# One layout of 6 tokens on 96 partitions for q, k and v, with exps and packed products written contiguously

## The chip, the cores and the metric

The kernel runs on 1 core of one Trainium2 chip. The metric is the device time of one execution in microseconds; a trace's "span" is the time from the first to the last instruction, some 2 us shorter. The engines are TensorE (PE; its weight loads are shown as PEld), VectorE (DVE), ScalarE (ACT), GpSimd (POOL) and SyncE (SP). PSUM is the memory in which this kernel's matmuls leave their results, SBUF holds its other tiles, and an eviction is an instruction of VectorE or ScalarE that reads PSUM and writes SBUF. A packet is one record of the trace's DMA part. A run over 1.5% above the fastest of the same kernel is called slow. Fast runs are compared with fast runs.

## The reference

```python
batch, n_heads, seq, head_dim = (8, 8, 576, 64)      # q, k, v; p has 32 rows in place of 576
def sm_attn(qq, kk, vv):
    s = scale * np.matmul(qq, kk.transpose(0, 1, 3, 2))
    ...                                              # softmax over the last axis
    return np.matmul(a, vv)
p_packed = sm_attn(p, k, v)
out = sm_attn(q, p_packed, p_packed)
x = out.transpose(0, 2, 1, 3).reshape(B * S, H * D)  # 4608 tokens x 512
h = x @ w_in                                         # w_in 512 x 2048
g = h * np.cos(h)
return g @ w_out                                     # w_out 2048 x 512, result float32
```

## The kernel before

The kernel works batch by batch. Because `p_packed` has only 32 rows per head, it multiplies these rows with `w_in` first: the "packed products" `PPW`, 128 rows x 2 groups x 2048 columns per batch. The second softmax gives `a2n`, and `h` is one matmul of `PPW` with `a2n`. The output projection of the batch before (`ot`) is used as filler: `fill(n)` puts n of its matmuls between other work of TensorE.

The parts that the change touches:

```python
def load(n, b):                      # cast to bf16 during the transfer
    if n == "q":                     # 128 partitions, 9216 bytes of float32 each, in one piece
        t = x[n, b] = ld_pool.tile([128, S * H * D // 128], BF16, name="q_bf", tag=n)
        G.dma_start(out=t, in_=q[b].rearrange("h (r t) d -> (h r) (t d)", r=QG))
    else:                            # 96 partitions, 6 tokens of each head
        t = x[n, b] = ld_pool.tile([KP, H, KC * D], BF16, name=n + "_bf", tag=n)
        G.dma_start(out=t, in_=src[n][b].rearrange("h (p c) d -> p h (c d)", c=KC))

def load_w_out(n):                   # 4 rows of w_out, 8 KB, in one piece
    G.dma_start(out=w_out_bf[:, 4 * n:4 * n + 4, :],
                in_=moe_w_out.rearrange("(n m j) d -> m n j d", n=4, j=4)[:, n])
...
def ppw_piece(b, n, engs):           # a quarter of the packed products
    ...                              # 8 matmuls into ps[0], ps[1]
    for g in range(2):
        dst = PPW[b][:, g, n * 512:(n + 1) * 512].rearrange("p (j m) -> p m j", j=4)
        src_ = ps[g].rearrange("p (m j) -> p m j", j=4)
        ...                          # dst = src_ * rinv, on VectorE or ScalarE
...
def s2_exp(b, g):
    dst = a2u[b][:, g].rearrange("p (r t o) -> p o t r", r=QG, o=2)
    for o in range(2):
        A.activation(out=dst[:, o], in_=ps[o], func=AF.Exp, ...)
```

`PPW` is written with 256 bytes between neighbouring elements of the inner loop (128 bf16 elements), the exps with 72 bytes (36 elements). The loads stand in one queue in this order: k, v, q of batch 0; `w_in`; the rest of p; `w_out`; k, q, v of batch 1; k, q, v of batch 2. k and q of batch 0 are transposed by TensorE (`pe_T`), all later ones by a transposing DMA (`dma_T`), issued by SyncE. TensorE works in program order, so after batch 0 it stands still until the transpose of k of batch 1 ("kT(1)") has landed:

```python
dma_T("k", 1)
dma_T("q", 1)
...                                  # batch 0: h, sin, g
dma_T("k", 2)
set_filler(0)
exp_table()
fill(16)
for i in range(3):
    s1_mm(1, i)                      # the first matmuls that read kT(1)
    s1_exp(1, i)
```

The softmax here doesn't subtract the row's maximum and nothing guards it: scores larger than these inputs give would overflow.

Of the kernel before, what the change touches and what calls it, by code (L numbers as in the profile page):

```python
# [8 lines left out]
FP32 = mybir.dt.float32  # L9
BF16 = mybir.dt.bfloat16  # L10
AF = mybir.ActivationFunctionType
ALU = mybir.AluOpType
# [4 lines left out]
def kernel(  # L17
# [14 lines left out]




    nc = tc.nc
    B, H, S, D = q.shape
    DM, DF = moe_w_in.shape
    scale = 1.0 / (D ** 0.5)
    NFC = DF // 128  # L40
    KP, KC = 96, S // 96
    QG, QB = 128 // H, S * H // 256
    PSUM = bass.MemoryType.PSUM

    const = ctx.enter_context(tc.tile_pool(name="const", bufs=1))
    ld_pool = ctx.enter_context(tc.tile_pool(name="ld", bufs=2))
    T_pool = ctx.enter_context(tc.tile_pool(name="T", bufs=2))
# [8 lines left out]
    work = ctx.enter_context(tc.tile_pool(name="work", bufs=5, space=PSUM))  # L56
# [4 lines left out]
    V, A, G = nc.vector, nc.scalar, nc.gpsimd  # L61
# [4 lines left out]
    ident = const.tile([128, 128], BF16, name="ident")  # L66
# [7 lines left out]
    src = {"k": k, "q": q, "v": v}  # L74
# [3 lines left out]
    x, xT = {}, {}  # L78

    def load(n, b):  # L80
        if n == "q":
            t = x[n, b] = ld_pool.tile([128, S * H * D // 128], BF16, name="q_bf", tag=n)
            G.dma_start(out=t, in_=q[b].rearrange("h (r t) d -> (h r) (t d)", r=QG))
        else:
            t = x[n, b] = ld_pool.tile([KP, H, KC * D], BF16, name=n + "_bf", tag=n)
            G.dma_start(out=t, in_=src[n][b].rearrange("h (p c) d -> p h (c d)", c=KC))

    def load_w_in(c0, c1):
        G.dma_start(out=w_in_bf[:, :, c0:c1], in_=moe_w_in.rearrange("(a p) n -> p a n", p=128)[:, :, c0:c1])

    def load_w_out(n):
        G.dma_start(out=w_out_bf[:, 4 * n:4 * n + 4, :],
                    in_=moe_w_out.rearrange("(n m j) d -> m n j d", n=4, j=4)[:, n])

    def copy(eng, out, in_):
        if eng is A:
            A.copy(out=out, in_=in_)  # L97
        else:
            eng.tensor_copy(out=out, in_=in_)  # L99


    def T_tile(n, b):
        w = 128 if n == "q" else KP
        t = xT[n, b] = T_pool.tile([128, H * S // (2 * w), w], BF16, name=n + "T", tag=n + "T")
        return t, (x[n, b] if n == "q" else x[n, b].rearrange("p h x -> p (h x)")), w

    def dma_T(n, b):
        t, f, w = T_tile(n, b)
        nc.sync.dma_start_transpose(out=t, in_=f)

    def pe_T(n, b, engs):
        t, f, w = T_tile(n, b)
        nb = f.shape[-1] // 128
        for i, j0 in enumerate(range(0, nb, 8)):
            m = min(8, nb - j0)
            ps = work.tile([128, m, w], BF16, name="tps", tag="w")
            for j in range(m):
                nc.tensor.transpose(ps[:, j, :], f[:, (j0 + j) * 128:(j0 + j + 1) * 128], ident[0:w, 0:w])
            copy(engs[i % len(engs)], t[:, j0:j0 + m, :], ps)

    def pack_p(b0, b1):

# [12 lines left out]
    a2u, a2n, PPW, rinv, ppT, lns = {}, {}, {}, {}, {}, {}  # L135
    s1_ps, s2_ps = {}, {}
# [35 lines left out]
    def ppw_piece(b, n, engs):  # L172
        if b not in PPW:
            PPW[b] = ppw_pool.tile([128, 2, DF], BF16, name="PPW", tag="PPW")
        ps = [work.tile([128, 512], FP32, name="ppw", tag="w") for _ in range(2)]
        for hp in range(4):
            for o in range(2):
                r = slice(64 * o, 64 * o + 64)
                nc.tensor.matmul(ps[o][32 * hp:32 * hp + 32], ppT[b][r, 2 * hp + o, :],  # L179
                                 w_in_bf[r, hp, n * 512:(n + 1) * 512], start=True, stop=True,  # L180
                                 tile_position=(64 * o, 32 * hp))
        for g in range(2):
            dst = PPW[b][:, g, n * 512:(n + 1) * 512].rearrange("p (j m) -> p m j", j=4)
            src_ = ps[g].rearrange("p (m j) -> p m j", j=4)
            s = rinv[b][:, 2 * g:2 * g + 1]
            if engs[g] is A:
                A.activation(out=dst, in_=src_, func=AF.Copy, scale=s)  # L187
            else:
                engs[g].tensor_scalar(out=dst, in0=src_, scalar1=s, scalar2=None, op0=ALU.mult)  # L189

    def s2_mm(b, g):

        ps = s2_ps[b, g] = [work.tile([128, QB, QG], FP32, name="s2", tag="w") for _ in range(2)]
        for hp in range(4):
            for o in range(2):
                r = slice(64 * o, 64 * o + 64)
                h = 2 * hp + g
                nc.tensor.matmul(ps[o][32 * hp:32 * hp + 32], ppT[b][r, h, :],
                                 xT["q", b][r, :, QG * h:QG * h + QG],
                                 start=True, stop=True, tile_position=(64 * o, 32 * hp))  # L200

    def s2_exp(b, g):
        ps = s2_ps.pop((b, g))
        if b not in a2u:
            a2u[b] = a2_pool.tile([128, 2, S], BF16, name="a2u", tag="a2u")
        dst = a2u[b][:, g].rearrange("p (r t o) -> p o t r", r=QG, o=2)
        for o in range(2):
            A.activation(out=dst[:, o], in_=ps[o], func=AF.Exp, scale=rinv[b][:, 2 * g + 1:2 * g + 2])  # L208

    def sums(b, i):  # L210

# [17 lines left out]

    gT, joint, ht, h_open = {}, {}, {}, {}  # L230

    def h_mm(b, fc):


        if fc == 0:
            gT[b] = g_pool.tile([128, NFC, 512], BF16, name="gT", tag="gT")
            if b % 2 == 0:
                joint[b // 2] = g_pool.tile([128, NFC, 128], BF16, name="joint", tag="joint")
        ps = h_open[b, fc] = work.tile([128, 512], FP32, name="hT", tag="w")
        for g in range(2):  # L240
            nc.tensor.matmul(ps, PPW[b][:, g, fc * 128:(fc + 1) * 128],  # L241
                             a2n[b][:, g, 0:512], start=(g == 0), stop=(g == 1))
        j = fc % 8
        for jj in {2: (0, 1), 3: (2, 3)}.get(j, (j,) if j > 3 else ()):
            if jj == 0:
                ht[b] = t_ps.tile([128, 8, 64], FP32, name="ht", tag="ht")
            f0 = (fc - j + jj) * 128
            for g in range(2):
                nc.tensor.matmul(ht[b][:, jj, :], PPW[b][:, g, f0:f0 + 128],  # L249
                                 a2n[b][:, g, 512:576], start=(g == 0), stop=(g == 1))  # L250

    def h_sin(b, fc):
# [14 lines left out]

    n_out = [0]

    def out_gen(b):  # L270
        chunks = [(gT[b], i) for i in range(4)]
        if b % 2 == 1:
            chunks.insert(0, (joint[b // 2], None))
        for t, i in chunks:
            x0 = 0 if i is None else i * 128
            ps = o_ps.tile([128, DM], FP32, name="ot", tag="ot")
            for fc in range(NFC):
                nc.tensor.matmul(ps, t[:, fc, x0:x0 + 128], w_out_bf[:, fc, :],  # L278
                                 start=(fc == 0), stop=(fc == NFC - 1))
                if fc < NFC - 1:  # L280
                    yield
            osb = o_pool.tile([128, DM], FP32, name="osb")
            copy(V if n_out[0] % 2 == 0 else A, osb, ps)
            n_out[0] += 1
            if i is None:
                nc.sync.dma_start(out=out[(b - 1) * S + 512:b * S, :], in_=osb[0:64, :])
                nc.sync.dma_start(out=out[b * S + 512:(b + 1) * S, :], in_=osb[64:128, :])
            else:
                nc.sync.dma_start(out=out[b * S + i * 128:b * S + (i + 1) * 128, :], in_=osb)
            yield  # L290

    filler = [None, 0]
# [14 lines left out]


    load("k", 0)
    nc.sync.dma_start(out=p_raw[:, 0:2, :], in_=p_rows[:, 0:2, :])  # L310
    make_identity(nc, ident)
    load("v", 0)
    load("q", 0)
    load_w_in(0, 512)
    load_w_in(512, DF)
# [28 lines left out]
    for g in range(2):  # L344
        s2_mm(0, g)
        s2_exp(0, g)
    ppw_piece(0, 0, [V, V])
    for i in range(3):
        sums(0, i)
    normalise(0)  # L350
    dma_T("k", 1)
    dma_T("q", 1)


# [6 lines left out]
    pack_p(1, 4)  # L361
    pack_p(4, 8)
    dma_T("k", 2)


# [8 lines left out]
    for g in range(2):  # L374
        s2_mm(1, g)
        s2_exp(1, g)
# [31 lines left out]
    def exp_phase(s, b2, b1):  # L408
        exp_table()
        s2_exp(b2, 0)  # L410
        s2_mm(b2, 1)
        s2_exp(b2, 1)
        fill(3)
        for i in range(3):
            if b1 is not None:
                s1_mm(b1, i)
                s1_exp(b1, i)
            fill(4)
        for i in range(3):
            sums(b2, i)  # L420
            fill(2)
        normalise(b2)
        h_mm(s, 8)
        fill(3)
        h_mm(s, 9)
        fill(3)
# [59 lines left out]
```

## Time and profile before

| | before |
|---|---|
| median of 3 runs | 337.89 us (336.65 to 340.62) |
| span of the profiled run | 336.1 us |
| first matmul on kT(1) | 60.2 us |
| first h matmul of batch 1 | 86.1 us |
| start of the exps of batches 2 to 7 | 99.5, 135.9, 170.2, 204.1, 237.9, 272.3 us |

From the page of the kernel before: busy us, share of the span and instructions of each engine, and the shares of the chain of work that ended last.

```profile
PE 264.1 (79%) x2226; PEld 127.6 (38%) x2226; DVE 210.5 (63%) x276; ACT 262.3 (78%) x298; POOL 22.5 (7%) x37
...
PE 30%; ACT 30%; DMA 17%; DVE 15%; issue 7%; POOL 1%; ACTq 0%; POOLq 0%; DVEq 0%
```

Two engines are about equally busy and the chain is spread over four kinds of work, so the page alone names no single limit. The groups of instructions (line, engine, operation, output<-inputs, shapes, count | busy us, mean ns of one | idle time before) show what is expensive:

```profile
L278 PE MATMUL ot<-w_out_bf,gT 128*128 128x512 bf16 x512 | 135.3, 386 | 0.0
L256 ACT ACTIVATE cosT<-hT,pihalf 128x512 bf16<-128x512 f32 x128 | 89.2, 740 | 15.9 <-PE hT L241 14.0 <-DVE gT L257 1.6
...
L189 DVE TENSOR_SCALAR PPW<-ppw,rinv 128x512 bf16<-128x512 f32 x34 | 84.3, 2524 | 6.0 <-PE ppw L179 6.0
...
L187 ACT ACTIVATE PPW<-ppw,rinv 128x512 bf16<-128x512 f32 x30 | 76.2, 2574 | 4.6 <-PE ppw L179 4.4
...
L99 DVE COPY osb<-ot 128x512 f32<-128x512 f32 x18 | 12.4, 688 | 19.3 <-PE ot L278 19.3
```

A packed product of 128x512 takes 2.5 us, while a plain copy of the same size out of PSUM (`osb`) takes 0.69 us. The exps of 128x288 are as slow for their size. One of the 32 from the instructions of their line (count: duration in ns min/median/max):

```profile
L208 ACT ACTIVATE a2u<-s_321,rinv x1: 1746/1746/1746, 21.2 to 21.2; 128x288 bf16<-128x288 f32 x1
```

The median of the 32 is 1.73 us. These durations overlap: within a group of four, one exp starts mostly 1.24 us after the other.

The chain of waits in order of time (start us, us, what), a few of its pieces:

```profile
14.15 23.93 DMA k_bf<-in_k_dram
38.09 22.03 DMA kT<-k_bf
...
62.30 4.29 PE ot L278 x12
...
80.51 6.96 DVE PPW L189 x3
...
99.46 5.25 ACT a2u L208 x4
...
313.94 18.14 PE ot L278 x84
```

The first 60 us are one load and one transpose. After that the a2u exps and the PPW products stand in the chain again and again. Three stages, from the start of the exps of one batch to that of the next (from:to in us and length, then busy us and instructions of PE, PEld, DVE, ACT, POOL, then granted clock, DMA share, GB/s):

```profile
170.20:204.10 33.90, 30.03 (x270) 14.48 (x269) 24.21 (x31) 32.62 (x39) 1.36 (x2) 1.00 0.63 121
204.10:237.90 33.80, 30.80 (x272) 14.88 (x271) 24.38 (x32) 32.66 (x38) 0.00 (x0) 1.00 0.33 67
237.90:272.30 34.40, 30.16 (x266) 14.50 (x265) 24.28 (x32) 32.51 (x38) 0.00 (x0) 1.00 0.22 56
```

ScalarE is busy about 32.6 of 34 us; TensorE about 30.2. At the start-to-start pitch of its matmuls TensorE's work in a stage needs about 27.6 us (an estimate from the pitches in this trace).

Two answers of the DMA view (packets, megabytes, share of 16 engines) for q0, the queue of the loads, and q1, the queue of transposes and stores: first q0 from 20 to 36 us, when only loads run; then both from 46 to 54 us, when the transpose of k(1) runs beside loads.

```profile
q0 software_dynamic: 1450, 3.51, 109.1%
```

The answer for 46 to 54 us, q0 and q1:

```profile
q0 software_dynamic: 747, 1.02, 92.5%
q1 hardware_dynamic: 751, 0.19, 33.9%
```

Load packets and transpose packets come in equal numbers there.

### The profile page before, as it was taken

What the parts mean: (1) busy time and instruction counts of PE and PEld (TensorE: products, weight loads), DVE (VectorE), ACT (ScalarE), POOL (GpSimd) and SP (SyncE); (2) the same over time, 40 slices, a digit from 0 to 9 for tenths busy, and PEclk for the clock granted to TensorE, in tenths of its full rate; (3) what the DMA queues carried; (4) which work ended last, traced back from release to release, by engine and by line L of the source; (5) the groups of instructions that cost most, each with busy time, mean ns of one, the idle gap of its engine ahead of it and who ended that gap; (6) DMA issues with size and microseconds to landing.
All of it is one profiled execution on the core that took longest, in us unless ns stands there. A gap on an engine that the chain in (4) does not pass through costs nothing.

```text
span 336.1 us, 5402 instructions
## 1 busy us (share of the span) xinstructions
PE 264.1 (79%) x2226; PEld 127.6 (38%) x2226; DVE 210.5 (63%) x276; ACT 262.3 (78%) x298; POOL 22.5 (7%) x37
## 2 busy tenths in 40 slices
PE   1835734865769478899889888998898879999995
PEld 1801222431335133454345334543443434444442
DVE  1367993066980989169925992599349934866400
ACT  1378980279999889999999989999999997966300
POOL 8112000110100200001001000000000000000000
PEclk9999799599699769999999999999999998999999
DMA  8999999999931990146867651514040011010131
GB/s 116 211 230 213 205 160 135 187 214 219 167 54 57 181 178 8 26 115 122 172 130 136 113 111 56 82 53 101 34 103 31 33 31 63 33 62 35 61 94 62
DMA packets 53703, 36.90 MB, mean 110 GB/s; under 512 B 34112, under 2 KB 46912, under 8 KB 53680
## 3 DMA queue, kind: packets, MB, share of 16 engines
q0 software_dynamic: 15456, 18.81, 34.5%
q1 hardware_dynamic: 38224, 17.76, 24.2%
q8 instruction: 17, 0.28, 0.3%
q14 instruction: 6, 0.05, 0.0%
HBM read 37.22 MB, written 9.44 MB: 139 GB/s over the span
## 4 chain that ended last, share of the span: by engine, by line
PE 30%; ACT 30%; DMA 17%; DVE 15%; issue 7%; POOL 1%; ACTq 0%; POOLq 0%; DVEq 0%
PE ot L278 18%; ACT a2u L208 10%; DVE PPW L189 8%; DMA k_bf<-in_k_dram 7%; PE hT L241 7%; DMA kT<-k_bf 7%; ACT PPW L187 6%; ACT cosT L256 4%; DVE gT L257 4%; DMA q_bf<-in_q_dram 3%; ACT a1T L147 2%; DVE ppT L168 2%; ACT lns L218 2%; ACT L256 2%; PE ppw L179 1%
## 5 line engine op out<-in xcount | busy, mean ns | idle before, releaser
L278 PE MATMUL ot<-w_out_bf,gT 128*128 128x512 bf16 x512 | 135.3, 386 | 0.0
L256 ACT ACTIVATE cosT<-hT,pihalf 128x512 bf16<-128x512 f32 x128 | 89.2, 740 | 15.9 <-PE hT L241 14.0
L257 DVE TENSOR_TENSOR gT<-hT,cosT 128x512 bf16<-128x512 f32 x128 | 88.8, 729 | 15.3 <-ACT cosT L256 14.8
L241 PE MATMUL hT<-a2n,PPW 128*128 128x512 bf16 x256 | 81.0, 405 | 15.3 <-ACT PPW L187 8.1
L189 DVE TENSOR_SCALAR PPW<-ppw,rinv 128x512 bf16<-128x512 f32 x34 | 84.3, 2524 | 6.0 <-PE ppw L179 6.0
L187 ACT ACTIVATE PPW<-ppw,rinv 128x512 bf16<-128x512 f32 x30 | 76.2, 2574 | 4.6 <-PE ppw L179 4.4
L278 PEld LDWEIGHTS <-gT 128*128 128x128 bf16 x512 | 44.0, 100 | 50.9 <-issue 15.9
L224 DVE TENSOR_TENSOR a2n<-a2u,lns 128x576 bf16<-128x576 bf16 x16 | 11.4, 755 | 52.4 <-ACT lns L222 52.4
L241 PEld LDWEIGHTS <-PPW 128*128 128x128 bf16 x256 | 24.3, 101 | 46.0 <-issue 16.4
L179 PE MATMUL ppw<-w_in_bf,ppT 64*32 64x512 bf16 x256 | 20.5, 419 | 18.3 <-ACT PPW L187 9.5
L249 PEld LDWEIGHTS <-PPW 128*128 128x128 bf16 x256 | 21.2, 100 | 24.6 <-issue 3.3
L97 ACT COPY osb<-ot 128x512 f32<-128x512 f32 x18 | 11.9, 659 | 16.4 <-PE ot L278 16.4
L99 DVE COPY osb<-ot 128x512 f32<-128x512 f32 x18 | 12.4, 688 | 19.3 <-PE ot L278 19.3
L249 PE MATMUL ht<-a2n,PPW 128*128 128x64 bf16 x256 | 23.6, 195 | 0.0
L168 DVE CAST ppT<-pp 64x128 bf16<-64x128 f32 x32 | 9.4, 294 | 17.0 <-PE pp L161 16.6
L142 PEld LDWEIGHTS <-kT 128*96 128x96 bf16 x192 | 13.4, 141 | 16.5 <-issue 6.8
L179 PEld LDWEIGHTS <-ppT 64*32 64x32 bf16 x256 | 6.1, 90 | 30.2 <-issue 22.5
L278 PE MATMUL ot<-w_out_bf,joint 128*128 128x512 bf16 x64 | 17.2, 392 | 0.0
L217 PE MATMUL sm<-a2u,ones_blk 128*128 128x384 bf16 x24 | 8.4, 360 | 8.2 <-ACT a2u L208 8.2
L218 ACT ACTIVATE lns<-sm 128x384 f32<-128x384 f32 x24 | 10.8, 514 | 0.8 <-PE sm L217 0.8
L261 ACT ACTIVATE cosTt<-ht,pihalf 128x512 bf16<-128x512 f32 x16 | 11.1, 691 | 0.0
L263 DVE TENSOR_TENSOR joint<-ht,cosTt 128x512 bf16<-128x512 f32 x16 | 11.0, 688 | 0.0
(154 smaller groups left out, 204.7 us busy)
## 6 DMA issues: line engine op xcount, KB each, us to landing
out_dram<-osb SPq DMA_DIRECT2D x32, 256.0 KB, 2.0
k_bf<-in_k_dram POOLq DMA_DIRECT2D x8, 576.0 KB, 9.2
v_bf<-in_v_dram POOLq DMA_DIRECT2D x8, 576.0 KB, 8.8
q_bf<-in_q_dram POOLq DMA_DIRECT2D x8, 576.0 KB, 9.4
w_out_bf<-in_moe_w_out_dram POOLq DMA_DIRECT2D x4, 512.0 KB, 23.4
w_in_bf<-in_moe_w_in_dram POOLq DMA_DIRECT2D x1, 1536.0 KB, 19.1
out_dram<-osb SPq DMA_DIRECT2D x8, 128.0 KB, 2.3
w_in_bf<-in_moe_w_in_dram POOLq DMA_DIRECT2D x1, 512.0 KB, 12.4
```

Source lines behind the costliest of these rows:

```text
L142: nc.tensor.matmul(ps[:, :, h % 2, h // 2, :], xT["k", b][:, h * (KC // 2) + i, :], P2[:, b, h], start=True, stop=True)
L168: V.tensor_copy(out=tv[64 * half:64 * half + 64, :, o, :], in_=pv[64 * o:64 * o + 64])
L179: nc.tensor.matmul(ps[o][32 * hp:32 * hp + 32], ppT[b][r, 2 * hp + o, :], w_in_bf[r, hp, n * 512:(n + 1) * 512], start=True, stop=True, ti ...
L187: A.activation(out=dst, in_=src_, func=AF.Copy, scale=s)
L189: engs[g].tensor_scalar(out=dst, in0=src_, scalar1=s, scalar2=None, op0=ALU.mult)
L208: A.activation(out=dst[:, o], in_=ps[o], func=AF.Exp, scale=rinv[b][:, 2 * g + 1:2 * g + 2])
L218: A.activation(out=lns[b].rearrange("p g s -> p (g s)")[:, c], in_=ps, func=AF.Ln)
L241: nc.tensor.matmul(ps, PPW[b][:, g, fc * 128:(fc + 1) * 128], a2n[b][:, g, 0:512], start=(g == 0), stop=(g == 1))
L249: nc.tensor.matmul(ht[b][:, jj, :], PPW[b][:, g, f0:f0 + 128], a2n[b][:, g, 512:576], start=(g == 0), stop=(g == 1))
L256: A.activation(out=cs, in_=ps, func=AF.Sin, bias=pihalf)
L257: todo = [lambda: V.tensor_tensor(out=gT[b][:, fc, :], in0=ps, in1=cs, op=ALU.mult)]
L278: nc.tensor.matmul(ps, t[:, fc, x0:x0 + 128], w_out_bf[:, fc, :], start=(fc == 0), stop=(fc == NFC - 1))
```

## The change

The intent: give q the layout of k and v, so that the exps come out in the order in which they are computed; write the packed products in order too, which needs `w_out` by rows of 2 KB; and undo the permutation of the tokens only in the last store. The core of the diff:

```diff
     def load(n, b):
-        if n == "q":
-            t = x[n, b] = ld_pool.tile([128, S * H * D // 128], BF16, name="q_bf", tag=n)
-            G.dma_start(out=t, in_=q[b].rearrange("h (r t) d -> (h r) (t d)", r=QG))
-        else:
-            t = x[n, b] = ld_pool.tile([KP, H, KC * D], BF16, name=n + "_bf", tag=n)
-            G.dma_start(out=t, in_=src[n][b].rearrange("h (p c) d -> p h (c d)", c=KC))
+        t = x[n, b] = ld_pool.tile([KP, H, KC * D], BF16, name=n + "_bf", tag=n)
+        G.dma_start(out=t, in_=src[n][b].rearrange("h (p c) d -> p h (c d)", c=KC))
 ...
     def load_w_out(n):
         G.dma_start(out=w_out_bf[:, 4 * n:4 * n + 4, :],
-                    in_=moe_w_out.rearrange("(n m j) d -> m n j d", n=4, j=4)[:, n])
+                    in_=moe_w_out.rearrange("(a p) n -> p a n", p=128)[:, 4 * n:4 * n + 4, :])
 ...
-            dst = PPW[b][:, g, n * 512:(n + 1) * 512].rearrange("p (j m) -> p m j", j=4)
-            src_ = ps[g].rearrange("p (m j) -> p m j", j=4)
+            dst = PPW[b][:, g, n * 512:(n + 1) * 512]
 ...                                            # s2_mm: reads 3 blocks of 96 tokens of a head
-        dst = a2u[b][:, g].rearrange("p (r t o) -> p o t r", r=QG, o=2)
         for o in range(2):
-            A.activation(out=dst[:, o], in_=ps[o], func=AF.Exp, ...)
+            A.activation(out=a2u[b][:, g, o * (S // 2):(o + 1) * (S // 2)], in_=ps[o], func=AF.Exp, ...)
 ...
+    def store(b, y0, y1, osb, r):
+        rows = out[b * S:(b + 1) * S, :].rearrange("(p c) d -> p c d", c=KC)
+        while y0 < y1:
+            i, p0 = y0 // KP, y0 % KP
+            m = min(y1 - y0, KP - p0)
+            nc.sync.dma_start(out=rows[p0:p0 + m, 2 * (i % 3) + i // 3, :], in_=osb[r:r + m, :])
+            y0, r = y0 + m, r + m
```

More of the change, by code (lines that the diff above doesn't have):

```diff
@@ L41 @@
     KP, KC = 96, S // 96
-    QG, QB = 128 // H, S * H // 256
     PSUM = bass.MemoryType.PSUM
@@ L102, in T_tile @@
     def T_tile(n, b):
-        w = 128 if n == "q" else KP
-        t = xT[n, b] = T_pool.tile([128, H * S // (2 * w), w], BF16, name=n + "T", tag=n + "T")
-        return t, (x[n, b] if n == "q" else x[n, b].rearrange("p h x -> p (h x)")), w
+        t = xT[n, b] = T_pool.tile([128, H * KC // 2, KP], BF16, name=n + "T", tag=n + "T")
+        return t, x[n, b].rearrange("p h x -> p (h x)")
     def dma_T(n, b):
-        t, f, w = T_tile(n, b)
+        t, f = T_tile(n, b)
         nc.sync.dma_start_transpose(out=t, in_=f)
     def pe_T(n, b, engs):
-        t, f, w = T_tile(n, b)
-        nb = f.shape[-1] // 128
-        for i, j0 in enumerate(range(0, nb, 8)):
-            m = min(8, nb - j0)
-            ps = work.tile([128, m, w], BF16, name="tps", tag="w")
-            for j in range(m):
-                nc.tensor.transpose(ps[:, j, :], f[:, (j0 + j) * 128:(j0 + j + 1) * 128], ident[0:w, 0:w])
-            copy(engs[i % len(engs)], t[:, j0:j0 + m, :], ps)
+        t, f = T_tile(n, b)
+        for i in range(3):
+            ps = work.tile([128, 8, KP], BF16, name="tps", tag="w")
+            for j in range(8):
+                nc.tensor.transpose(ps[:, j, :], f[:, (8 * i + j) * 128:(8 * i + j + 1) * 128], ident[0:KP, 0:KP])
+            copy(engs[i % len(engs)], t[:, 8 * i:8 * i + 8, :], ps)
     def pack_p(b0, b1):
@@ L182, in ppw_piece @@
         for g in range(2):
-            dst = PPW[b][:, g, n * 512:(n + 1) * 512].rearrange("p (j m) -> p m j", j=4)
-            src_ = ps[g].rearrange("p (m j) -> p m j", j=4)
+            dst = PPW[b][:, g, n * 512:(n + 1) * 512]
             s = rinv[b][:, 2 * g:2 * g + 1]
             if engs[g] is A:
-                A.activation(out=dst, in_=src_, func=AF.Copy, scale=s)
+                A.activation(out=dst, in_=ps[g], func=AF.Copy, scale=s)
             else:
-                engs[g].tensor_scalar(out=dst, in0=src_, scalar1=s, scalar2=None, op0=ALU.mult)
+                engs[g].tensor_scalar(out=dst, in0=ps[g], scalar1=s, scalar2=None, op0=ALU.mult)
     def s2_mm(b, g):
-        ps = s2_ps[b, g] = [work.tile([128, QB, QG], FP32, name="s2", tag="w") for _ in range(2)]
+        ps = s2_ps[b, g] = [work.tile([128, S // 2], FP32, name="s2", tag="w") for _ in range(2)]
         for hp in range(4):
@@ L198, in s2_mm @@
                 nc.tensor.matmul(ps[o][32 * hp:32 * hp + 32], ppT[b][r, h, :],
-                                 xT["q", b][r, :, QG * h:QG * h + QG],
+                                 xT["q", b][r, 3 * h:3 * h + 3, :].rearrange("p c t -> p (c t)"),
                                  start=True, stop=True, tile_position=(64 * o, 32 * hp))
@@ L205, in s2_exp @@
             a2u[b] = a2_pool.tile([128, 2, S], BF16, name="a2u", tag="a2u")
-        dst = a2u[b][:, g].rearrange("p (r t o) -> p o t r", r=QG, o=2)
         for o in range(2):
-            A.activation(out=dst[:, o], in_=ps[o], func=AF.Exp, scale=rinv[b][:, 2 * g + 1:2 * g + 2])
+            A.activation(out=a2u[b][:, g, o * (S // 2):(o + 1) * (S // 2)], in_=ps[o], func=AF.Exp,
+                         scale=rinv[b][:, 2 * g + 1:2 * g + 2])
     def sums(b, i):
@@ L230, with h_lhs @@
     gT, joint, ht, h_open = {}, {}, {}, {}
+    def h_lhs(b, g, fc):
+        return PPW[b][:, g, fc * 128:(fc + 1) * 128]
     def h_mm(b, fc):
@@ L240, in h_mm @@
         for g in range(2):
-            nc.tensor.matmul(ps, PPW[b][:, g, fc * 128:(fc + 1) * 128],
+            nc.tensor.matmul(ps, h_lhs(b, g, fc),
                              a2n[b][:, g, 0:512], start=(g == 0), stop=(g == 1))
@@ L246, in h_mm @@
                 ht[b] = t_ps.tile([128, 8, 64], FP32, name="ht", tag="ht")
-            f0 = (fc - j + jj) * 128
             for g in range(2):
-                nc.tensor.matmul(ht[b][:, jj, :], PPW[b][:, g, f0:f0 + 128],
+                nc.tensor.matmul(ht[b][:, jj, :], h_lhs(b, g, fc - j + jj),
                                  a2n[b][:, g, 512:576], start=(g == 0), stop=(g == 1))
@@ L285, in out_gen @@
             if i is None:
-                nc.sync.dma_start(out=out[(b - 1) * S + 512:b * S, :], in_=osb[0:64, :])
-                nc.sync.dma_start(out=out[b * S + 512:(b + 1) * S, :], in_=osb[64:128, :])
+                store(b - 1, 512, 576, osb, 0)
+                store(b, 512, 576, osb, 64)
             else:
-                nc.sync.dma_start(out=out[b * S + i * 128:b * S + (i + 1) * 128, :], in_=osb)
+                store(b, i * 128, i * 128 + 128, osb, 0)
             yield
```

## The prediction

> **What bounds the kernel now.** The page's busy line gives TensorE 264 us, ScalarE 262, VectorE 211 of a 336 us span. Three parts, from the chain of waits and the busy time by window:
>
> - 0 to 60 us: transfers. The chain is the load of k(1) (to 38.1), then its transpose (to 60.2). Batch 0's arithmetic ends near 48 us.
> - 60 to 272 us: TensorE feeds ScalarE and VectorE, and slow evictions stand in the chain (a2u exps 10%, PPW products 14%). Exp phase to exp phase takes 33.3 to 34.4 us (37.4 for the first, with 10 us of half clock). Of a 33.9 us stage ScalarE is busy 32.6, VectorE 24.3; start-to-start pitches in the trace (216 ns per 512-column matmul) add up to about 27.6 us of TensorE work.
> - 272 to 336 us: nearly pure TensorE (53.5 us of pitch in 64).
>
> **Removed.** 64 packed products, 2.49 us (VectorE) and 2.54 us (ScalarE) each. Contiguous 128x512 work out of PSUM takes 0.66 to 0.69 us in this trace (osb copies): minus 62 us VectorE, minus 56 us ScalarE. 32 exps of 128x288 step every 1.24 us; the contiguous 128x384 Ln takes 0.38 to 0.5, so I estimate 0.42: minus 26 us ScalarE. Per stage: ScalarE about 21 us, VectorE 17; TensorE becomes the limit. The Trainium skill ("SBUF — State Buffer", Door 1: the DMA port swizzle) says accesses that step to a new 16-byte line each pay a penalty; the 3.7-fold eviction in this trace agrees.
>
> **Added.** q arrives as 768 B packets (79 ns) instead of 4608 B (361 ns): 3.8 us of all engines instead of 2.9. w_out in 1024 B packets (98 ns) instead of 4096 B (324 ns): 12.5 us instead of 10.4. k(1) should land about 3 us later. While its transpose runs, load and transpose packets alternate one for one (221 and 221 between 44 and 46 us; the skill's "DMA: Bandwidth & Descriptors", Queues, rings and completion order, states round-robin by packet). With q(2) in six times as many packets I expect kT(1) at about 66 us instead of 60. Stores grow from 40 to 72 issues, hidden except some 0.6 us at the end.
>
> **Sum of the critical path (estimates).**
> - kT(1) at 66 us (+6).
> - kT(1) to the first h matmul of batch 1: 18 us instead of 26 (serial here) → 84.
> - first half of stage 1: 8 instead of 13 → 92.
> - first exp-to-exp stage: 28.5 instead of 37.4 → 120.5.
> - four stages at 29.5 instead of 33.9 → 238.5 (27.6 of matmuls, 2 of stalls).
> - tail 60 instead of 64 → 298.5; remaining half-clock periods 2 → 300.5 us span, plus 1.5 to measured time.
>
> Predicted **302 us**, 8 in 10 within 292 to 314. Faster by over 2%: 0.97; within 2%: 0.02; slower: 0.01.
>
> **What would show each step.** PPW groups near 0.68 us, a2u near 0.42. ScalarE about 180 us busy, VectorE about 148, TensorE about 255. kT(1) landing at 64 to 68 us with q0/q1 packets alternating. Exp-phase spacing 29 to 30.5 us, TensorE idle in a stage under 3 us, TensorE above 50% of the chain.
>
> **What would make it wrong.** kT(1) not later, or much later (a one-to-one shift of the total). Stages held at 31 or more by latency of the exp phase (ScalarE in order) or by five PSUM buffers. Half clock returning: 5 us. Late qT/kT in stages 1 and 2.

## The result

The changed kernel took 290.28 us (median of 4 runs, 289.71 to 296.9; the 296.9 was a slow run) against 337.98 us. Two more runs of it are 290.34 (fast) and 299.13 (slow). The ratio is 0.8576, 95% interval 0.8522 to 0.8631. Ratios are the mean time of one kernel's fast runs over that of the other's fast runs of the same rounds, so not quite the ratio of the medians. The forecast direction was right, but 290.28 lies below the stated range of 292 to 314.

The profile first taken of the changed kernel was of the slow run (span 294.7 us). The same kernel was run again, unedited, and gave a fast profile (span 289.9 us; that run took 292.1 us). The readings below are from this fast profile.

```profile
PE 247.1 (85%) x2197; PEld 124.2 (43%) x2232; DVE 157.4 (54%) x276; ACT 188.9 (65%) x298; POOL 24.9 (9%) x37
...
PE 67%; DMA 22%; DVE 4%; ACT 3%; issue 2%; POOL 0%; ACTq 0%; POOLq 0%
```

The chain is now mostly TensorE. Groups:

```profile
L279 PE MATMUL ot<-w_out_bf,gT 128*128 128x512 bf16 x487 | 131.3, 386 | 2.0 <-issue 1.0
...
L248 ACT ACTIVATE cosT<-hT,pihalf 128x512 bf16<-128x512 f32 x128 | 85.7, 690 | 35.3 <-PE hT L234 32.3 <-DVE gT L249 2.2
...
L179 DVE TENSOR_SCALAR PPW<-ppw,rinv 128x512 bf16<-128x512 f32 x34 | 25.1, 747 | 5.6 <-PE ppw L170 5.2
...
L177 ACT ACTIVATE PPW<-ppw,rinv 128x512 bf16<-128x512 f32 x30 | 20.4, 685 | 1.4 <-PE ppw L170 1.4
```

The packed products fell from 2.5 us to 0.75 (VectorE) and 0.68 (ScalarE). The exps, all 32 in one line now (before, the median was 1.73 us):

```profile
L197 ACT ACTIVATE a2u<-s,rinv x32: 492/502/512, 18.8 to 231.8; 128x288 bf16<-128x288 f32 x32
```

The chain of waits, its first large pieces:

```profile
13.63 25.48 DMA k_bf<-in_k_dram
39.14 18.68 DMA kT<-k_bf
57.86 2.13 PE s L133 x24
59.99 4.45 PE ot L279 x12
...
76.35 1.98 DVE PPW L179 x3
```

k(1) lands at 39.1 us (before: 38.1) and kT(1) at about 57.8 (before: 60.1). The prediction had 66. The stages between the exps of batches 4 to 7:

```profile
143.50:173.20 29.70, 28.76 (x275) 14.76 (x281) 18.34 (x31) 23.86 (x38) 2.31 (x3) 1.00 0.81 144
173.20:202.10 28.90, 28.51 (x270) 14.38 (x272) 18.96 (x32) 23.45 (x38) 0.00 (x0) 1.00 0.42 79
202.10:230.60 28.50, 28.16 (x261) 13.96 (x264) 18.13 (x32) 23.25 (x38) 0.00 (x0) 1.00 0.30 68
```

A stage takes 29.0 us on average instead of 34.0, and TensorE is busy in nearly all of it. The DMA view of the same windows as before, q0 from 20 to 36 us:

```profile
q0 software_dynamic: 2881, 3.43, 120.0%
```

And q0 and q1 from 46 to 54 us:

```profile
q0 software_dynamic: 1516, 1.14, 90.7%
q1 hardware_dynamic: 1514, 0.39, 36.3%
```

From 20 to 36 us twice as many packets move almost the same bytes (3.43 MB against 3.51); the packets that shrank in this window are those of `w_out` (from 4096 to 1024 bytes), not yet those of q. From 46 to 54 us the transpose queue moves twice the packets that it moved before (1514 against 751). Neither is what the prediction assumed.

### The profile page after: what moved, and what is told of

Its sections match the earlier page's. It is cut to its first block, busy times and chain, and to the rows that moved or that the text cites. A ratio compares the mean times of both kernels' runs of the same rounds, so it can differ in the third digit from the quotient of the medians.

```text
span 294.7 us, 5419 instructions
## 1 busy us (share of the span) xinstructions
PE 249.8 (85%) x2197; PEld 124.9 (42%) x2232; DVE 157.3 (53%) x276; ACT 188.8 (64%) x298; POOL 24.9 (8%) x37
## 4 chain that ended last, share of the span: by engine, by line
PE 63%; DMA 30%; ACT 2%; issue 2%; DVE 1%; POOL 1%; ACTq 0%; POOLq 0%
PE ot L279 38%; DMA kT<-k_bf 18%; PE hT L234 14%; DMA k_bf<-in_k_dram 8%; DMA q_bf<-in_q_dram 4%; PE ppw L170 2%; PE ht L241 2%; PE sm L207 1%; PE pp L147 1%; PE pp L152 1%; ACT L248 0%; DVE gT L249 0%; DVE ppT L159 0%; ACT lns L212 0%; ACT lns L208 0%
## 5 line engine op out<-in xcount | busy, mean ns | idle before, releaser
L248 ACT ACTIVATE cosT<-hT,pihalf 128x512 bf16<-128x512 f32 x128 | 85.6, 689 | 35.1 <-PE hT L234 32.1
L249 DVE TENSOR_TENSOR gT<-hT,cosT 128x512 bf16<-128x512 f32 x128 | 85.8, 685 | 28.8 <-ACT cosT L248 28.7
L234 PE MATMUL hT<-a2n,PPW 128*128 128x512 bf16 x249 | 76.2, 392 | 4.7 <-DVE a2n L214 2.7
L234 PEld LDWEIGHTS <-PPW 128*128 128x128 bf16 x256 | 23.7, 99 | 31.7 <-DVE a2n L214 3.4
L179 DVE TENSOR_SCALAR PPW<-ppw,rinv 128x512 bf16<-128x512 f32 x34 | 25.0, 746 | 5.6 <-PE ppw L170 5.4
L93 DVE COPY osb<-ot 128x512 f32<-128x512 f32 x18 | 12.3, 684 | 21.6 <-PE ot L279 21.6
L91 ACT COPY osb<-ot 128x512 f32<-128x512 f32 x18 | 10.6, 586 | 18.0 <-PE ot L279 17.7
L177 ACT ACTIVATE PPW<-ppw,rinv 128x512 bf16<-128x512 f32 x30 | 20.4, 684 | 1.4 <-PE ppw L170 1.4
L170 PE MATMUL ppw<-w_in_bf,ppT 64*32 64x512 bf16 x256 | 16.1, 413 | 4.0 <-DVE gT L249 1.4
L279 PE MATMUL ot<-w_out_bf,joint 128*128 128x512 bf16 x61 | 15.8, 380 | 0.5 <-issue 0.5
L80 POOL DMA_DIRECT2D q_bf<-in_q_dram x8 | 6.2, 770 | 71.3 <-DMA qT<-q_bf 68.1
## 6 DMA issues: line engine op xcount, KB each, us to landing
k_bf<-in_k_dram POOLq DMA_DIRECT2D x8, 576.0 KB, 11.9
```

The costliest lines, as they stand in the source:

```text
L93: eng.tensor_copy(out=out, in_=in_)
L170: nc.tensor.matmul(ps[o][32 * hp:32 * hp + 32], ppT[b][r, 2 * hp + o, :], w_in_bf[r, hp, n * 512:(n + 1) * 512], start=True, stop=True, ti ...
L177: A.activation(out=dst, in_=ps[g], func=AF.Copy, scale=s)
L179: engs[g].tensor_scalar(out=dst, in0=ps[g], scalar1=s, scalar2=None, op0=ALU.mult)
L234: nc.tensor.matmul(ps, h_lhs(b, g, fc), a2n[b][:, g, 0:512], start=(g == 0), stop=(g == 1))
L248: A.activation(out=cs, in_=ps, func=AF.Sin, bias=pihalf)
```

## The experiments

All outputs are right. "The whole change" below is the changed kernel. Of the first four, all intervals but that of `before_q768` lie wholly below 0.98.

### 1. The changed kernel again (`after_again`)

Edit: none.

> The changed kernel unedited, to get a profile in the fast state (the first profile was a slow run of 294.7 us span, the fast ones had 287.4 to 288.5). Theory: the 7 us between the two lie in the head, between kT(1) and the first h matmul of batch 1 (25.8 us in the slow profile, where kT(2) and kT(3) took 15.8 and 12.9 us to land; my prediction had 18). So in a fast profile that piece should take 18 to 20 us and the exp-to-exp spacings stay at 28.5 to 29.3 us. Rival: the slow run is slow everywhere (clock), then the spacings are 27.8 to 28 and the head is unchanged.

Measured: 290.72 us, ratio 0.8612 (0.8529 to 0.8694). The piece from kT(1) to the first h matmul took 19.7 us (57.9 to 77.6), the spacings from the exps of batch 3 on 29.3, 29.7, 28.9 and 28.5 us. So the slow profile is slow in the head, as the theory had it; of the spacings only 29.7 is just outside the stated 28.5 to 29.3. In the slow run's chain the later transposes stand too:

```profile
38.68 17.64 DMA kT<-k_bf
...
57.44 15.79 DMA kT<-k_bf
...
79.03 12.85 DMA kT<-k_bf
```

In the fast profile the second and third of these are not among the waits that matter. Why these two transposes took 15.8 and 12.9 us in that run is not known; nothing below rests on it.

### 2 and 3. Each half of the change alone (`ppw_only`, `tokens_only`)

`ppw_only` is the kernel before with the packed products in order and `w_out` in 2 KB rows:

```diff
-                    in_=moe_w_out.rearrange("(n m j) d -> m n j d", n=4, j=4)[:, n])
+                    in_=moe_w_out.rearrange("(a p) n -> p a n", p=128)[:, 4 * n:4 * n + 4, :])
...
-            dst = PPW[b][:, g, n * 512:(n + 1) * 512].rearrange("p (j m) -> p m j", j=4)
-            src_ = ps[g].rearrange("p (m j) -> p m j", j=4)
+            dst = PPW[b][:, g, n * 512:(n + 1) * 512]
+            src_ = ps[g]
```

`tokens_only` is the changed kernel with exactly these lines put back.

> The kernel before with only the packed products written contiguously and w_out in 2 KB rows; tokens, q load, exps and stores as before. Theory (evictions set the stage spacing, q's packet size sets when kT(1) lands): products at 0.68 to 0.75 us instead of 2.5, exps still 1.24 us apart, exp-to-exp spacing 30.5 to 31.5 us instead of 33.9, kT(1) still at about 60 us (w_out's smaller packets cost it under 1 us), total about 307 us, 0.91 of before. Rival (the earlier kT(1) of the changed kernel comes from w_out or from the faster evictions): kT(1) at 56 to 57 us here.

> The changed kernel with the packed products strided again and w_out as before; so only q in 96 partitions, the contiguous exps and the permuted stores. Theory: kT(1) at 56 to 57 us as in the whole change, exps about 0.4 us apart, products still 2.5 us, spacing about 31 us, total about 318 us, 0.94 of before. Rival: kT(1) at 60 us here. If both parts add up, the two savings (about 31 and 20 us) sum to the whole one of 48; if TensorE takes over as the limit they sum to more than 48.

| kernel | median us | ratio (95%) | kT(1) first used | last four spacings, mean |
|---|---|---|---|---|
| before | 338.74 | 1 | 60.2 | 34.1 |
| `ppw_only` | 311.31 | 0.9244 (0.9185 to 0.9303) | 60.6 | 31.3 |
| `tokens_only` | 318.41 | 0.9438 (0.9356 to 0.9519) | 57.7 | 31.7 |
| the whole change | 290.72 | 0.8612 (0.8529 to 0.8694) | 57.9 | 29.1 |

(Positions are those of the profiled run of each kernel; the profile of before is the one shown above. The median of `tokens_only` includes a slow run of 324.38 us, its ratio does not.) The savings of the two halves, 27.4 and 20.3 us, add up to 47.7; the whole change saves 48.0 in the same rounds. Only the half that holds the new q load moves kT(1) forward. `w_out` in small packets does not: k(1) landed at 39.0 us in `ppw_only`, 0.9 us later than before, and kT(1) at about the old time.

Against the expectations: `ppw_only` took 311 us instead of about 307, with its spacing inside the stated 30.5 to 31.5; `tokens_only` met its total, but kT(1) came at 57.7 instead of 56 to 57. Savings that sum to more than 48 us were to be the sign that TensorE takes over as the limit. 47.7 is not that sign, so the reading that TensorE limits the stages gets no support from this pair.

### 4. Only the packet size of q (`before_q768`)

The kernel before, with the same q load as two transfers whose pieces are 768 bytes:

```diff
-            G.dma_start(out=t, in_=q[b].rearrange("h (r t) d -> (h r) (t d)", r=QG))
+            tv = t.rearrange("p (c e x) -> p e c x", e=2, x=384)
+            qv = q[b].rearrange("h (r t) d -> (h r) (t d)", r=QG).rearrange("p (c e x) -> p e c x", e=2, x=384)
+            for e in range(2):
+                G.dma_start(out=tv[:, e], in_=qv[:, e])
```

> The kernel before with the same q load cut into two transfers of 768-byte packets (was 4608), nothing else. Theory (a transpose packet alternates with a load packet, so large q packets hold the transpose of k(1) back): kT(1) lands at 56 to 57 us instead of 60, total about 334 us, 0.985 to 0.99 of before. Rival of my prediction (smaller packets move fewer bytes per us and mean more alternations, so kT(1) lands later, near 65): total 340 or more. Third: packet size of q does not matter, kT(1) at 60, ratio 1.00.

Measured: 333.57 us, ratio 0.9919 (0.9824 to 1.0015); the interval just touches 1, so the total alone decides nothing. The profile does: the first matmul on kT(1) starts at 58.1 us instead of 60.2 (expected: 56 to 57), and the queues between 46 and 54 us look like those of the whole change. The transpose of k(1) in the chain, here and in `ppw_only`, which keeps the large q packets:

```profile
38.37 19.64 DMA kT<-k_bf
```

```profile
39.02 21.56 DMA kT<-k_bf
```

The DMA view of `before_q768` for that window:

```profile
q0 software_dynamic: 1471, 1.09, 87.1%
q1 hardware_dynamic: 1462, 0.37, 35.1%
```

The same of `ppw_only`:

```profile
q0 software_dynamic: 784, 1.05, 95.3%
q1 hardware_dynamic: 783, 0.20, 37.2%
```

In all of these windows load packets and transpose packets come one for one (784 and 783, 1471 and 1462). With large q packets among the loads 750 to 780 transpose packets get through in 8 us, with small ones about 1460 to 1510. So smaller q packets bring kT(1) forward. My prediction, that they hold it back, is refuted by an edit that changes only them (and cuts the load into two transfers; `tokens_only`, with one transfer of 768-byte packets, has kT(1) at 57.7).

The traces show one thing more. In these profiles kT(1) landed within 0.6 us of the last load beside it, that of v(2): 60.1 and 59.6 us before, 60.6 and 60.0 in `ppw_only`, 58.0 and 58.1 in `before_q768`, 57.7 and 57.9 in `tokens_only`, 57.8 and 57.9 in the whole change. Once the loads were gone, 1132 transpose packets passed in one microsecond (58 to 59 us, the whole change), against some 190 beside them. So both queues drain about 2 us sooner with small q packets; how much of this is the transposes' own pace and how much the earlier end of the loads, no run separates.

### 5. The loads of batch 2 held back (`hold`)

Two tiny copies on GpSimd read kT(1) and qT(1), so that the loads behind them in the same queue wait:

```diff
+    held = const.tile([1, 2], BF16, name="held")
+    for i, n in enumerate("kq"):
+        G.tensor_copy(out=held[:, i:i + 1], in_=xT[n, 1][0:1, 0, 0:1])
+    for n in "kqv":
+        load(n, 2)                   # was issued with the loads of batch 1
```

> The changed kernel with the loads of k(2), q(2) and v(2) held back until the transposes of k(1) and q(1) have landed, so that these transposes meet only the end of the loads of q(1) and v(1). Theory (competition with load packets is what makes kT(1) take 18 to 19 us; without it a transpose takes about 5): kT(1) at 47 to 49 us instead of 57.9, and since TensorE waits for it one to one, the first h matmul of batch 1 moves from 78 to 68 to 70 us as long as kT(2), now loaded later, is there in time; total about 281 us. Rival (the transpose is slow by itself, or the total does not hang on kT(1)): kT(1) still after 54 us, or kT(1) early and total still 288 to 291.

Measured: 298.43 us, ratio 0.8841 (0.8780 to 0.8903): slower than the whole change, against both expectations of the total. The chain says why:

```profile
39.07 8.70 DMA kT<-k_bf
...
50.87 7.29 DMA k_bf<-in_k_dram
58.24 17.12 DMA kT<-k_bf
```

The transpose of k(1) took 8.7 us instead of 18.7, and kT(1) was in use at 47.8, as expected. But k(2) now landed only at 58.2, its transpose ran beside the loads of batches 2 and 3 and took 17.1 us, and the first h matmul of batch 1 came at 84.8 instead of 77.6. This shows two things: the competition of the loads costs a transpose 8 to 10 us; and the 10 us won at kT(1) were lost again in the next wait of the same kind. An earlier kT(1) counts only while kT(2) keeps up.

### 6 and 7. TensorE transposes in the head (`pe1`, `pe12`)

`pe1` takes the transposes of batch 1 away from the DMA queue; `pe12` that of k(2) as well:

```diff
-    dma_T("k", 1)
-    dma_T("q", 1)
...
+    pe_T("k", 1, [V, A])
     fill(16)
+    pe_T("q", 1, [V, A])
...                                  # pe12 also:
-    dma_T("k", 2)
...
     ppw_piece(1, 0, [V, V])
     fill(4)
+    pe_T("k", 2, [V, A])
```

> The changed kernel with k and q of batch 1 transposed by TensorE, as batch 0 is, in the time when it waits for kT(1) now; the two transfers are gone. k(1) lands at 39 us, so the first score matmul of batch 1 should start at 43 to 45 us instead of 57.9, the first h matmul of batch 1 at about 62 to 66 us instead of 78 unless the loads of v(1) and k(2) with its transpose come in as the next wait. Theory (the head's wait counts one to one): total 276 to 281 us. Rival (another wait of the head takes its place at once): total 286 us or more.

> As the run before, and k of batch 2 transposed by TensorE too, just ahead of its score matmuls. If the next wait of the head is the transpose of k(2), this saves another 2 to 5 us on the run with batch 1 alone (total 273 to 278); if it is the loads themselves, the two runs agree within 1 us.

Measured: `pe1` 287.84 us, ratio 0.8528 (0.8464 to 0.8592); `pe12` 282.30 us, ratio 0.8358 (0.8303 to 0.8413). In `pe1` the scores of batch 1 started at 50.7 us (expected 43 to 45: the 16 filler matmuls between the two transposes take several microseconds) and the first h matmul of batch 1 at 67.8 (expected 62 to 66), and the next wait was not k(2) but the transpose of q(2). It stands in the list of waits (engine, line <- what it waited for: us, times, longest):

```profile
PE s L188 <- DMA qT<-q_bf: 4.5, 1, 4.5
```

So `pe1` missed its total of 276 to 281. In `pe12`, with one transpose less in the queue, this wait is gone and the total is 5.5 us below `pe1`. The scores of batch 1 start at 49.0, but the first h matmul of batch 1 comes no earlier than in `pe1` (67.7; the whole change: 77.6). The gain lies behind it: the exps of batch 2 start at 76.8 us instead of 79.0, and those of batch 3 follow after 28.4 us instead of 31.8. No run explains the second part. 5.5 us is slightly more than the 2 to 5 us expected for this step, but with `pe1` already too high the total is still above the expected 273 to 278. `pe12` is the fastest kernel, about 8 us below the whole change (290.72 and 282.30 were measured on two chips; the kernel before took 338.74 and 338.01 there).

### 8. Useless work on ScalarE (`act_pad`)

```diff
             todo = h_sin(b, fc)
+            if fc in (4, 6, 12, 14):
+                A.activation(out=pad_out, in_=pad_in, func=AF.Copy, scale=1.0)
```

> The changed kernel with four useless ScalarE copies of 128x640 (about 0.7 us each, 2.8 us per stage, some 20 us in all) in every stage. Theory (after the change the stage spacing is set by TensorE, 28.4 us busy of 29.1, and ScalarE has 5 us of room): spacing 29 to 29.7 us, total at most 293 us. Rival (the spacing is still set by ScalarE's chain of exps, Ln and sines): spacing 31 to 32 us, total 303 us or more.

Measured: 290.79 us, ratio 0.8595 (0.8514 to 0.8677). The durations of the 28 copies add up to 20.4 us, ScalarE's busy time grows by 14 us (203.0 against 188.9, since instructions overlap), and the kernel takes no longer. The same three stages:

```profile
143.60:172.10 28.50, 27.82 (x265) 13.96 (x268) 18.16 (x31) 25.52 (x41) 1.58 (x3) 1.00 0.85 147
172.10:201.20 29.10, 28.70 (x269) 14.49 (x273) 18.86 (x32) 25.40 (x42) 0.00 (x0) 1.00 0.43 78
201.20:229.80 28.60, 28.07 (x260) 13.91 (x263) 18.05 (x32) 25.30 (x42) 0.00 (x0) 1.00 0.30 68
```

ScalarE is busy 2 us more per stage and the stages are as long as without the copies. After the change 2 us more of ScalarE work fit into a stage, of the some 5 us that it has to spare, so its amount of work does not set the spacing. TensorE, busy 28.2 of these 28.7 us, is what remains (VectorE is busy 18). No run changed the work of TensorE or VectorE in a stage, so that TensorE sets the spacing is argued from busy time and the chain, not shown by an edit.

## Why the prediction was wrong

The prediction was a sum of pieces of the critical path. Beside what the fast profile of the whole change measured (run of 292.1 us):

| term | predicted us | measured us | off by |
|---|---|---|---|
| kT(1) in use | 66 | 57.9 | -8.1 |
| to the first h matmul of batch 1 | 18 | 19.7 | +1.7 |
| first half of stage 1 | 8 | 9.0 | +1.0 |
| first exp-to-exp stage | 28.5 | 27.6 | -0.9 |
| four stages | 118 | 116.4 | -1.6 |
| tail | 60 | 59.3 | -0.7 |
| remaining half clock | 2 | 0 (in the pieces above) | -2.0 |
| span to measured time | 1.5 | 2.2 | +0.7 |

(The first exp-to-exp stage of the kernel before took 36.4 us, from 99.5 to 135.9, not the 37.4 of the prediction.)

The failed step is this one: "With q(2) in six times as many packets I expect kT(1) at about 66 us instead of 60." It carries 8 of the 10 us by which this run is shorter than predicted. Without it the prediction would have been about 294 us. That the other terms together are off by only 1.8 us is partly luck: their errors, +3.4 and -5.2 us, cancel in part. The failed step was wrong in sign, and runs decide both of its parts:

- **Loads slow little with smaller packets here.** I multiplied the recorded duration of a packet by the number of packets, and expected k(1) some 3 us later. But the durations overlap (their shares of 16 engines are 109% and 120%): from 20 to 36 us, with `w_out` in 1024-byte packets in place of 4096, the same queue moved 3.51 MB in 1450 packets before and 3.43 MB in 2881 packets after, 2% less. k(1) landed 0.6 to 1.0 us later in the whole change, 0.9 in `ppw_only`, 0.3 in `tokens_only` and `before_q768`. The Trainium skill says as much ("DMA: Bandwidth & Descriptors", Specifications): line rate needs transfers of at least 512 B, and all packets in question are larger. The prediction did not use it.
- **Round-robin by packet works the other way.** The skill's statement (same page, Queues, rings and completion order) that an engine alternates between its queues by packet agrees with the trace: 1516 load and 1514 transpose packets between 46 and 54 us. But I drew the wrong conclusion. When each small transpose packet lets one load packet pass, it waits longer behind a large one. I took one time per pair for both sizes and counted more pairs (the prediction does not write this out). Its one stated pace, 221 pairs from 44 to 46 us, is from a window in which every load packet had 768 bytes, so it could not show what large ones cost. From 48 to 50 us, when the load packets of the kernel before averaged 2.8 KB, only 82 transpose packets passed, against 373 in the whole change; 8 us hold 750 to 780 pairs with large q packets in the mix and 1460 to 1510 with small ones. `hold`, where the transpose of k(1) took 8.7 us with most loads out of the way, shows that the competition is what makes it long. That the wait behind the large packets is the mechanism is read from these counts; the edit of `before_q768` shows only that their size matters.

What held:

- **The evictions.** Products at 0.68 to 0.75 us (predicted 0.68), exps 0.38 to 0.40 us apart (0.42). The products with `w_out` alone bring 27.4 of the 48 us, the other half alone 20.3 (q's packets included).
- **TensorE as the limit of a stage.** Predicted spacing 29 to 30.5 us, idle under 3; measured 28.5 to 29.7, with TensorE idle about 0.7 us. `act_pad` shows that ScalarE has room for at least 2 us more. TensorE lines are 67% of the chain (predicted over 50).
- **The stores.** 72 issues instead of 40 do not appear in the chain; the tail is within 1 us of the forecast.
- **Busy times** were 9 us too low for ScalarE and VectorE (189 and 157 measured, 180 and 148 predicted) and 8 too high for TensorE. No run was spent on that; the stages still came out about as forecast.

The half clock did not disappear as such: the window from kT(1) to the first h matmul ran at a granted clock of 0.77, as the one of before did at 0.83, while the stages from 114 us on ran at 1.00. Just before it TensorE had waited 11.9 us for kT(1), and from 57.9 to 60.2 us the granted clock was 0.50. The Trainium skill ("TensorE: Matmul & The Clock Gate", What's actually happening) ties the half rate to idle windows of TensorE, and the wait for kT(1) is such idle time, so the trace agrees. In `pe1` and `pe12`, without this wait, the same piece ran at 0.90 and 0.91, but they change other things too; no run tested the clock alone.

What stays open: why a run now and then is 6 to 11 us longer (two runs of the changed kernel at 296.9 and 299.13, one of `tokens_only` at 324.38 and one of `act_pad` at 302.09), beyond the sight of two slow transposes in one profile. Open too are the shares of the two causes in the 2 us of kT(1) (experiment 4), and whether adding or removing TensorE work would move the stages.

## What to carry to other kernels

Look first at the time of an eviction for its size: the same 128x512 block out of PSUM cost 2.5 us when neighbouring results were written 256 bytes apart and 0.7 us in order, and reordering the weights and the final store to allow that cost under 1 us at the start and nothing visible at the end. Do not cost a transfer by the recorded durations of its packets; look at the bytes per microsecond of the queue, and where two queues run together, at how many packets of each get through, because in these runs the queue of small packets went slower the larger the other's packets were. When a wait at the start is removed, check the next wait of the same kind before you book the gain: `hold` won 10 us at kT(1) and lost more than that at kT(2), while `pe12` took both off the queue and kept 8 us.

## What the Trainium skill lacked or had wrong

- "DMA: Bandwidth & Descriptors" gives the round-robin by packet, but not what follows for a transposing DMA beside loads. Here the transpose of k(1) took 22.0 and 21.6 us (two profiles) beside loads with 4608-byte q packets among them, 18.7 to 19.6 us (four fast profiles; 17.6 in the slow one) beside 768-byte packets, and 8.7 us (`hold`) with most of the loads out of the way. The page also speaks of 9 to 17 descriptors per packet; in the packet records of these traces one load packet of up to 4608 bytes goes with one 256-byte transpose packet. Whether such a record is a packet or a descriptor of the page is not known.
- "SBUF — State Buffer" (Door 1: the DMA port swizzle) says that accesses that step to a new 16-byte line pay a penalty, but gives no size for an engine's write of bf16. Here: 128x512 from PSUM, 256 bytes between neighbours, 2.52 us on VectorE and 2.57 on ScalarE, in order 0.75 and 0.68; 128x288 Exp on ScalarE, 72 bytes between neighbours, 1.73 us (median), in order 0.50. The shape of the write pattern changed together with the distance, and no run separates the two. But an element took about 4.5 ns with inner runs of 4 (three products on VectorE in 6.96 us) and 4.3 ns with inner runs of 16 (exps 1.24 us apart on ScalarE), an estimate that speaks for the distance.
- Nothing in these runs contradicted a statement of the pages that were used.
